# Two transformer layers on one core: block 0's projections by token tile, two single loads of X, normalization on either of two engines, and a new order list

## The chip, the cores and the metric

The kernel runs on one core of a Trainium2 chip. The metric is the device time of one execution in microseconds (us); the time of a version is the median of its runs. The engines are PE (TensorE: matmuls, and PEld for its weight loads), DVE (VectorE), ACT (ScalarE), POOL (GpSimd) and SP (SyncE, which here only issues DMAs). Each has its own queue and works through it in order.

## The reference

The input is a sequence of 2,048 tokens of 512 bf16 values. Two layers follow, with the same weights:

```python
x = x + A(layernorm(x))      # attention
x = x + B(layernorm(x))      # MLP
x = x + A(layernorm(x))
x = x + B(layernorm(x))

# A: qkv = x @ wqkv; 32 heads of 16; scores = q k^T / 4
mask = (i - j >= 0) & (i - j < 256)       # a sliding, causal window
p = softmax(where(mask, scores, -1e9));  return (p v) @ wo
# B: gelu_tanh(x @ w1 + b1) @ w2 + b2,  512 -> 1792 -> 512
```

The layer normalization has no weights: mean and variance over the 512 values, eps 1e-5.

## The kernel before, in words

**Tiles and blocks.** X lies in SBUF as 16 tiles of 128 tokens. The two layers are run as one stream of 32 token tiles (number 0 to 31; 16 is tile 0 in the second layer), in 16 blocks of two tiles. Within a block there are these steps:

- `layernorm` (L720): DVE takes statistics of a tile (L727, L729), adds eps (L731), POOL raises to -1/2 (L734), and DVE subtracts the mean and scales (L737). That normalized row is transposed by four PE transposes into PSUM and copied out by ACT or DVE (`evac`, L711), or, for most tiles ahead of the MLP, by DVE and DMAs through a scratch tensor (L746 to L755).
- `lnq` (L787): both tiles of a block, then Q. `proj` (L808) makes Q or K for two of the four channel blocks of 128 in one PSUM bank, with matmuls of 256 columns, that is both token tiles at once. Each reads both transposed tiles of the block (`xr`).
- `kv` (L815): K by `proj`, copied out by one DVE instruction for two channel blocks, which also separates the even from the odd heads (L824); V with matmuls of 512 columns per tile (L834).
- `attention` (L860): the scores of a block are cut into visits of 512 columns. A visit is one group of PE matmuls of 32 rows (label S below), and two exponentials of 128 x 1024 on ACT (L903). The edges of the window are masked by multiplications on DVE or POOL (L924). `pv` (L929) multiplies by V in two halves per two channel blocks, transposes and divides on DVE (and partly POOL, L994). `outproj` (L1024) follows, with the addition to X on DVE (L784), the second layer normalization, and the addition of b2 on POOL (L1033).
- `mlp` (L1046): ten jobs of two or four tiles; W1, Gelu on ACT (L1069, or in pairs by DVE and ACT at L1058 and L1061), W2 (L1076) with 14 matmuls of 512 columns for a tile, the addition to X (L784) and, in the second layer, the store of the tile (L1081).

**Loads.** SP issues, one behind the other: X tiles 0 and 1, 2 and 3, 4 to 7, b1, Wo, X tiles 8 to 15, W1, W2, b2 (L698 to L706). ACT's queue issues the three parts of Wqkv (L694). Until data is there, PE clears PSUM banks with 8 and then 5 matmuls of 512 columns on zeros (L676).

**What sets the order.** Every instruction or small group becomes a numbered node by `add`. `ORDER` (L413) is a written-out list of all node numbers; it gives each engine the order of its queue, SP's DMAs too. `TURNS` chooses, for each node that may run on two engines (`alt`), which one it takes: copies on DVE or ACT, masks and divisions on DVE or POOL. `BANKS` names the PSUM bank or banks of each node that takes some. `_List.run` (L231) goes through the list and puts times on the nodes by a cost model (constants L188 to L192; `CODE` is for the fetching of PE's instructions); these times only decide where waits are put (`_Sched.spread`, L135), not the order. A node's waits stand in its own engine's queue, so what is behind a waiting node waits as well.

Where PE goes from one shape of matmul to another (full 128 x 128, the 32-row scores, the 17-column products with V) this text speaks of a change of shape.

Of the kernel before, what the change touches and what calls it, by code (L numbers as in the profile page):

```python
# [185 lines left out]
class _List:  # L186
# [5 lines left out]
    CODE = (194.0, 256.0, 2.006, 3400.0)  # L192
# [106 lines left out]
def bass_interleave_layers__sliding_block__dense_activation_gelu__prompt_kernel(  # L299
# [72 lines left out]
    with ExitStack() as kctx:  # L372
        S_ = _Sched(nc, kctx)

        def sb(name, shape, dtype=dt.bfloat16):
# [774 lines left out]
```

## Time and profile before

| what | before |
|---|---|
| median of 3 runs | 457.03 us (456.97 to 457.27) |
| the profiled execution | 460.18 us |
| its span, first to last instruction | 458.4 us |
| mean granted TensorE clock | 0.993 |
| PE idle waits of the kind "issue" (released by nothing that the profile shows) | 2.2 us, the longest 1.7 |
| first projection, first exponential | 9.09, 15.51 us |
| last matmul's result taken up by DVE | 455.54 us |
| exponentials (L903): count, busy | 304, 286.3 us |
| masks (L924) on POOL, on DVE | 133, 129 |
| instruction packets (queue q8) | 69, 1.13 MB |

The times inside the profile are of the profiled execution; it takes 3.15 us longer than the median of the unprofiled runs. A row of the table of stretches gives, for each engine, the busy time and in brackets the number of instructions, then the clock that was granted to PE, the share of the DMA engines and the GB/s. A row of the chain of waits has its start, its length and what it was.

### The profile page before, as it was taken

To read this page: it belongs to the slowest core of one execution; us is meant where nothing else is said; L and a number is where in the kernel's file an instruction comes from. 1 tells how busy PE (TensorE), PEld (TensorE's weight loads), DVE (VectorE), ACT (ScalarE), POOL (GpSimd) and SP (SyncE) were. 2 spreads that over 40 slices of the span, in tenths; PEclk is the share of its full clock that TensorE was granted. 3 is DMA by queue.
4 is the path that set the end of the run, shared out by engine and by line. 5 is a ranking of instruction groups with operands and counts; after the bars stand their busy time and mean duration, and the time that the engine had idled before them with its cause. 6 is when DMAs were issued, how large, how long until landed. Compare 5 with 4: busy or idle time off the path is not lost.

```text
span 458.4 us, 19422 instructions
## 1 busy us (share of the span) xinstructions
PE 444.1 (97%) x8790; PEld 238.7 (52%) x8790; DVE 368.5 (80%) x749; ACT 389.7 (85%) x462; POOL 234.7 (51%) x266
## 2 busy tenths in 40 slices
PE   7999999989899999999999999999999999999997
PEld 3655655645453554645455545546464554545664
DVE  5899988999777888989889888899788888677411
ACT  2899999999789999899997999889987999792442
POOL 5377666565768266332565467754355243462400
PEclk9999999999989999999999999999999999999999
DMA  8910000001110020100120000201012002201211
GB/s 271 370 62 4 4 3 3 4 3 26 40 35 1 9 44 9 43 3 11 21 68 3 5 23 15 60 9 24 3 23 58 3 11 52 72 2 33 67 52 36
DMA packets 27839, 18.17 MB, mean 40 GB/s; under 512 B 15852, under 2 KB 27244, under 8 KB 27756
## 3 DMA queue, kind: packets, MB, share of 16 engines
q1 hardware_dynamic: 26172, 15.35, 12.8%
q8 instruction: 69, 1.13, 1.1%
q10 hardware_dynamic: 1584, 1.57, 1.0%
q14 instruction: 14, 0.11, 0.1%
HBM read 11.41 MB, written 5.51 MB: 37 GB/s over the span
## 4 chain that ended last, share of the span: by engine, by line
PE 75%; ACT 21%; DVE 1%; DMA 1%; issue 1%
PE ps L32 74%; ACT E L903 16%; ACT gT L1069 2%; ACT gT L1061 1%; PE ps L36 1%; ACT L903 1%; ACT L1061 1%; DMA X<-in_A_x_dram 1%; DVE stat L727 0%; DVE X L784 0%; DVE xn L737 0%; ACT xnTA L715 0%; DVE statmv L729 0%; DVE veps L731 0%
## 5 line engine op out<-in xcount | busy, mean ns | idle before, releaser
L903 ACT ACTIVATE E<-ps 128x1024 bf16<-128x1024 f32 x304 | 286.3, 1048 | 24.9 <-PE ps L32 24.1
L924 POOL TENSOR_TENSOR E<-E,mask 128x512 bf16<-128x512 bf16 (+1 forms) x133 | 140.3, 1070 | 91.8 <-DVE E L924 46.9
L32 PE MATMUL ps<-W_sb,gT 128*128 128x512 bf16 x448 | 120.1, 380 | 0.0
L32 PE MATMUL ps<-xnTB,W_sb 128*128 128x512 bf16 (+1 forms) x560 | 113.1, 337 | 0.0
L32 PE MATMUL ps<-xnTA,Wqkv_sb 128*128 128x256 bf16 x512 | 76.3, 279 | 1.2 <-ACT xnTA L715 0.7
L32 PEld LDWEIGHTS ps<-xnTB,W_sb 128*128 128x128 bf16 x560 | 51.6, 98 | 43.4 <-ACT E L903 3.9
L784 DVE TENSOR_TENSOR X<-X,ps 128x512 bf16<-128x512 bf16 x64 | 43.3, 681 | 33.9 <-PE ps L32 33.0
L1069 ACT ACTIVATE gT<-ps,b1T 128x512 bf16<-128x512 f32 (+1 forms) x92 | 48.5, 588 | 23.9 <-PE ps L32 23.4
L32 PE MATMUL ps<-QT,KT 32*64 32x320 bf16 (+4 forms) x2976 | 65.7, 259 | 2.9 <-ACT E L903 1.2
L734 POOL TENSOR_TENSOR rstd<-veps,mhalf 128x1 f32<-128x1 f32 x64 | 36.2, 572 | 52.2 <-DVE veps L731 50.4
L32 PEld LDWEIGHTS ps<-W_sb,gT 128*128 128x128 bf16 x448 | 39.6, 98 | 42.2 <-issue 8.4
L32 PEld LDWEIGHTS ps<-xnTA,Wqkv_sb 128*128 128x128 bf16 x512 | 47.2, 100 | 23.9 <-issue 3.1
L32 PEld LDWEIGHTS ps<-QT,KT 32*64 32x64 bf16 x2976 | 27.6, 103 | 51.1 <-ACT E L903 32.3
L924 DVE TENSOR_TENSOR E<-E,mask 128x512 bf16<-128x512 bf16 (+1 forms) x129 | 51.1, 424 | 2.5 <-ACT E L903 2.5
L32 PE MATMUL ps<-E,Va 64*17 64x128 bf16 (+3 forms) x3872 | 49.3, 230 | 3.5 <-issue 1.7
L1033 POOL TENSOR_TENSOR X<-X,b2b 128x512 bf16<-128x512 bf16 x32 | 36.6, 1153 | 30.0 <-DVE TM L994 12.4
L989 DVE STREAM_TRANSPOSE TT<-ps 128x1024 f32<-128x1024 f32 x32 | 39.9, 1248 | 13.8 <-PE ps L32 13.1
L32 PEld LDWEIGHTS ps<-E,Va 64*17 64x17 bf16 x3872 | 39.5, 85 | 19.1 <-PE ps L32 6.3
L727 DVE BATCH_NORM_STATS2 stat<-X 128x6 f32<-128x512 bf16 x64 | 43.0, 678 | 3.9 <-DMA X<-in_A_x_dram 3.4
L824 DVE TENSOR_TENSOR KT<-ps,parmask 128x1024 bf16<-128x1024 f32 x32 | 38.6, 1206 | 1.3 <-PE ps L32 1.2
L1058 DVE TENSOR_SCALAR gT<-ps,b1T 128x512 bf16<-128x512 f32 (+1 forms) x48 | 31.8, 672 | 6.9 <-PE ps L32 6.3
L32 PE MATMUL ps<-Wqkv_sb,xnTA 128*128 128x512 bf16 x128 | 36.8, 381 | 0.5 <-issue 0.5
(49 smaller groups left out, 330.0 us busy)
## 6 DMA issues: line engine op xcount, KB each, us to landing
W_sb<-in_B_w_dram SPq DMA_DIRECT2D x2, 1792.0 KB, 17.5
scr_x<-xs_ SPq DMA_DIRECT2D x104, 32.0 KB, 1.6
xnTB<-scr_x SPq DMA_DIRECT2D x26, 128.0 KB, 2.8
out_dram<-X SPq DMA_DIRECT2D x16, 128.0 KB, 1.7
Wqkv_sb<-in_A_wqkv_dram ACTq DMA_DIRECT2D x3, 512.0 KB, 7.5
X<-in_A_x_dram SPq DMA_DIRECT2D x1, 1024.0 KB, 12.2
X<-in_A_x_dram SPq DMA_DIRECT2D x2, 256.0 KB, 4.6
X<-in_A_x_dram SPq DMA_DIRECT2D x1, 512.0 KB, 8.8
```

The lines of the kernel that those rows point to most:

```text
L32: return self.e.matmul(*a, **k)
L727: add("dve", lambda e, B: e.bn_stats(stat6[:, k6, :], X[:, t, :]), 590, reads=["X%d" % t], writes=["st%d" % k6], prio=prio)
L734: add("pool", lambda e, B: e.tensor_tensor(out=rstd[:, k : k + 1], in0=veps[:, k : k + 1], in1=mhalf[:], op=ALU.pow), 535, reads=["ve%d" % ...
L784: add("dve", lambda e, B: e.tensor_tensor(out=X[:, t, :], in0=X[:, t, :], in1=ps[:, B[g][0], :], op=ALU.add), d_psum(512), reads=["X%d" % ...
L824: add("dve", lambda e, B, g=g, i=i: e.tensor_tensor(out=KT[:, kb, :, 2 * i : 2 * i + 2, :].rearrange("p a c q -> p a (c q)"), in0=ps[:, B[ ...
L903: add("act", lambda e, B, g_=g_, gi=gi: e.activation(E[:, 2 * gi : 2 * gi + 2, e0 : e0 + 512], ps[:, B[g_][0] : B[g_][0] + 2, :], AF.Exp, ...
L924: op = lambda e, B, Ew=Ew, Mw=Mw: e.tensor_tensor(out=Ew, in0=Ew, in1=Mw, op=ALU.mult)
L989: add("dve", lambda e, B: e.transpose(TT[:, s].rearrange("p a c q d -> p a (c q d)"), ps[:, B[g][0] : B[g][0] + 2, :].rearrange("p a n -> ...
L1033: add("pool", lambda e, B: e.tensor_tensor(out=X[:, t, :], in0=X[:, t, :], in1=b2b[:], op=ALU.add), 1110, reads=["X%d" % t, "b2b"], writes ...
L1058: add("dve", lambda e, B, g=g, fc=fc: e.tensor_scalar(out=gT[:, fc, 0:M], in0=ps[:, B[g][0], 0:M], scalar1=b1T[:, fc : fc + 1], scalar2=No ...
L1061: add("act", lambda e, B, fcs=fcs: e.activation(gT[:, fcs[0] : fcs[-1] + 1, 0:M], gT[:, fcs[0] : fcs[-1] + 1, 0:M], AF.Gelu_apprx_tanh, sc ...
L1069: add("act", lambda e, B, g=g, fc=fc: e.activation(gT[:, fc, 0:M], ps[:, B[g][0], 0:M], AF.Gelu_apprx_tanh, bias=b1T[:, fc : fc + 1], scal ...
```

## The change

1. **Block 0's Q and K.** For block 0 only, each of the four channel blocks gets a PSUM bank of its own, and its matmuls are done per token tile: 128 columns for tile 0, which wait only for the transposed tile 0, and 128 columns for tile 1. There are 64 matmuls of 128 columns in the place of 32 of 256, four copies of Q of 256 columns in the place of two of 512, and four K copies of half the width in the place of two.
2. **Loads.** X 0 and X 1 are two DMAs. The second group of clearing matmuls has 7 in the place of 5.
3. **Normalization.** The subtract-and-scale of L737 may run on POOL; the new `TURNS` puts 39 of 64 there.
4. **Last tile.** W2 for tile 31 is done in two halves of 256 columns, each with its own bank, addition and store.
5. **Lists.** `ORDER`, `TURNS` and `BANKS` are new; two constants of the cost model's `CODE` and several landing times that it assumes are changed. With the new `TURNS`, 119 masks are on POOL and 143 on DVE, 22 divisions on POOL and 10 on DVE (19 and 13 before).

PE's queue in the new order begins with: 8 and 7 clears; transposes of tile 0; Q's channel blocks 0, 3 and 2 for tile 0; transposes of tile 1; Q 1, K 0 and K 1 for tile 0; Q 3, K 0 and Q 1 for tile 1; transposes of tiles 3 and 2; Q 2, K 1 and Q 0 for tile 1; block 1's first Q; V 0; the first score visit. Behind that comes K's channel blocks 2 and 3, between visits. ACT's queue has the copies of tiles 0, 1 and 3, four copies of Q, one of block 1's Q, and then the exponentials. DVE normalizes tile 0, POOL tile 1, DVE tiles 3 and 2.

```diff
-    CODE = (194.0, 256.0, 2.006, 3400.0)
+    CODE = (194.0, 256.0, 2.0090, 3700.0)
...
-        for n, took in ((8, 3420.0), (5, 1300.0)):
+        for n, took in ((8, 3420.0), (7, 1730.0)):
...
-        load_x(0, 2, 3300.0)
-        load_x(2, 2, 5500.0)
+        load_x(0, 1, 3200.0)
+        load_x(1, 1, 3600.0)
+        load_x(2, 2, 5700.0)
...
-            add("dve", lambda e, B: e.tensor_scalar(
+            scale = lambda e, B: e.tensor_scalar(
                 out=xn[:, s, :], in0=X[:, t, :], scalar1=statmv[:, k, 0:1], scalar2=rstd[:, k : k + 1],
...
+            add("dve", scale, 325, reads=["X%d" % t, "mv%d" % k, "rs%d" % k], writes=["xn%d" % s], prio=prio, lock=True,
+                alt=(("pool", scale, 760.0),))
...
+            if b == 0:
+                for kc in range(DC):
+                    g = "q0_%d" % kc
+                    prio = base + pair[kc // 2]
+                    first_proj(g, 0, kc, prio)
+                    evac(lambda B, kc=kc: QT[:, kc, 0:256], lambda B, g=g: ps[:, B[g][0], 0:256], 256,
+                         ["ps:" + g], ["Q0_%d" % kc], prio, free=[g], kind="q", boot=True)
+                return
...
+        def first_proj(g, which, kc, prio):
+            for j in range(2):
+                pe_group(g, [(Wqkv_sb[:, dc, which * D + kc * P : which * D + (kc + 1) * P], xnTA[:, 0, dc, j * P : (j + 1) * P],
+                              slice(j * P, (j + 1) * P), dc == 0, dc == DC - 1) for dc in range(DC)],
+                         P, DC, ["xa0_%d" % j, "Wqkv%d" % which], prio, fresh=(j == 0))
...
+            for kc in range(DC if b == 0 else 0):
+                g = "k0_%d" % kc
+                prio = kprio + pair[kc // 2]
+                first_proj(g, 1, kc, prio)
+                add("dve", lambda e, B, g=g, kc=kc: e.tensor_tensor(
+                    out=KT[:, 0, :, kc, :], in0=ps[:, B[g][0], 0:256][:, None, :].to_broadcast([P, 2, 256]),
+                    in1=parmask[:, :, None].to_broadcast([P, 2, 256]), op=ALU.mult), d_psum(512) + 10,
...
+        def last_tile(tau, i, prio):
+            t = tau % T
+            for half in range(2):
+                g = "y%d_%d" % (tau, half)
+                n = slice(half * D // 2, (half + 1) * D // 2)
+                pe_group(g, [(gT[:, fc, i * P : (i + 1) * P], W2_sb[:, fc, n], slice(0, D // 2), fc == 0, fc == FC - 1) for fc in range(FC)],
+                    D // 2, 1, [["g%d" % fc, "W2"] for fc in range(FC)], prio)
+                add("dve", lambda e, B, g=g, n=n: e.tensor_tensor(out=X[:, t, n], in0=X[:, t, n], in1=ps[:, B[g][0], 0 : D // 2], op=ALU.add),
...
+                dma(lambda e, B, n=n: e.dma_start(out[0, t * P : (t + 1) * P, n], X[:, t, n]),
```

More of the change, by code (lines that the diff above doesn't have):

```diff
@@ L692, in load_x @@
                 ["X%d" % t for t in range(t0, t0 + n)], lands)
-        for which, lands in enumerate((4700.0, 7500.0, 10400.0)):
+        for which, lands in enumerate((4900.0, 7900.0, 10800.0)):
             load(lambda e, B, which=which: e.dma_start(
@@ L697, in bass_interleave_layers__sliding_block__dense_activation_gelu__prompt_kernel @@
                 A_wqkv[:, which * D : (which + 1) * D].rearrange("(c p) n -> p c n", p=P)), ["Wqkv%d" % which], lands, eng="act")
-        load_x(0, 2, 3300.0)
-        load_x(2, 2, 5500.0)
-        load_x(4, 4, 9500.0)
-        load(lambda e, B: e.dma_start(b1raw[:], B_b1.rearrange("(c p) -> c p", p=P)), ["b1raw"], 9800.0)
-        load(lambda e, B: e.dma_start(Wo_sb[:], A_wo.rearrange("(c p) n -> p c n", p=P)), ["Wo"], 11500.0)
+        load_x(0, 1, 3200.0)
+        load_x(1, 1, 3600.0)
+        load_x(2, 2, 5700.0)
+        load_x(4, 4, 9700.0)
+        load(lambda e, B: e.dma_start(b1raw[:], B_b1.rearrange("(c p) -> c p", p=P)), ["b1raw"], 10000.0)
+        load(lambda e, B: e.dma_start(Wo_sb[:], A_wo.rearrange("(c p) n -> p c n", p=P)), ["Wo"], 11800.0)
         load_x(8, 8, 14700.0)
@@ L736, in layernorm @@
                 reads=["ve%d" % k, "mhalf"], writes=["rs%d" % k], prio=prio - 500)
-            add("dve", lambda e, B: e.tensor_scalar(
+            scale = lambda e, B: e.tensor_scalar(
                 out=xn[:, s, :], in0=X[:, t, :], scalar1=statmv[:, k, 0:1], scalar2=rstd[:, k : k + 1],
-                op0=ALU.subtract, op1=ALU.mult), 325,
-                reads=["X%d" % t, "mv%d" % k, "rs%d" % k], writes=["xn%d" % s], prio=prio, lock=True)
+                op0=ALU.subtract, op1=ALU.mult)
+            add("dve", scale, 325, reads=["X%d" % t, "mv%d" % k, "rs%d" % k], writes=["xn%d" % s], prio=prio, lock=True,
+                alt=(("pool", scale, 760.0),))
             g = "tp%d" % k
@@ L819, in kv @@
             xr = ["xa%d_0" % xs, "xa%d_1" % xs]
-            for i in range(DC // 2):
+            for kc in range(DC if b == 0 else 0):
[5 more added lines that the diff above has]
+                    in1=parmask[:, :, None].to_broadcast([P, 2, 256]), op=ALU.mult), d_psum(512) + 10,
+                    reads=["ps:" + g, "parmask"], writes=["K0_0_%d" % kc, "K0_1_%d" % kc], prio=prio, free=[g])
+            for i in range(DC // 2 if b else 0):
                 g = "k%d_%d" % (b, i)
@@ L1074, in mlp @@
                 tau = tau0 + i
+                if tau == NT - 1:
+                    last_tile(tau, i, prio2 + i)
+                    continue
                 g = "y%d" % tau
@@ L1082, in mlp @@
                         ["OUT%d" % t], reads=["X%d" % t], dur=2000.0, prio=prio2)
+        def last_tile(tau, i, prio):
[6 more added lines that the diff above has]
+                add("dve", lambda e, B, g=g, n=n: e.tensor_tensor(out=X[:, t, n], in0=X[:, t, n], in1=ps[:, B[g][0], 0 : D // 2], op=ALU.add),
+                    d_psum(D // 2), reads=["X%d" % t, "ps:" + g], writes=["XL%d" % half], prio=prio, free=[g])
+                dma(lambda e, B, n=n: e.dma_start(out[0, t * P : (t + 1) * P, n], X[:, t, n]),
+                    ["OUT%d_%d" % (t, half)], reads=["XL%d" % half], dur=1900.0, prio=prio)
         lnq(0, -1300, (20, 800))
```

424 rows, old and new, of tables (BANKS, ORDER, TURNS) are left out of this document.

## The prediction

> **What bounds the kernel now.** I read the page first, then the chain of waits, then the table of stretches, then the timeline of the two ends.
>
> ```profile
> span 458.4 us, 19422 instructions
> ...
> PE 444.1 (97%) x8790; PEld 238.7 (52%) x8790; DVE 368.5 (80%) x749; ACT 389.7 (85%) x462; POOL 234.7 (51%) x266
> ```
>
> PE is busy nearly always, but a busy PE need not stream at full rate, so the chain decides:
>
> ```profile
> 21.16 27.61 ACT E L903 x30
> ...
> 122.87 0.87 PE ps L32 x51
> 123.75 1.73 issue
> 125.47 2.11 PE ps L32 x24
> ...
> 156.40 1.03 ACT E L903
> 157.44 0.04 issue
> 157.48 2.40 PE ps L32 x55
> ```
>
> Up to about 157 us the end hangs mostly on ACT's exponentials; behind that it is PE alone. In between PE stands still for 1.73 us, and nothing that the profile shows releases it. The stretches:
>
> ```profile
> 6.05:9.46 3.41, 1.70 (x15) 0.81 (x14) 3.27 (x13) 1.19 (x2) 1.65 (x4) 1.00 1.09 349
> 9.46:12.87 3.41, 3.41 (x23) 2.61 (x21) 1.54 (x4) 0.60 (x1) 1.37 (x2) 0.50 1.10 350
> 20.00:50.00 30.00, 28.21 (x695) 16.36 (x693) 29.17 (x60) 29.91 (x34) 20.45 (x21) 1.00 0.19 60
> ...
> 122.00:125.50 3.50, 1.77 (x127) 1.21 (x103) 1.20 (x3) 1.64 (x3) 3.14 (x4) 1.00 0.34 73
> 125.50:128.90 3.40, 3.40 (x65) 2.21 (x65) 2.11 (x4) 1.94 (x2) 1.23 (x3) 0.50 0.53 134
> ...
> 160.00:420.00 260.00, 259.24 (x5398) 133.33 (x5396) 220.89 (x440) 231.90 (x261) 129.96 (x141) 1.00 0.12 25
> ```
>
> The columns are PE, PEld, DVE, ACT, POOL, the granted clock and the DMA. Two places lose time to something other than work. Twice a stretch of about 3.4 us with PE busy for only half of it (1.70 of 3.41, 1.77 of 3.50) is followed by 3.4 us at clock 0.50. From 20 to 50 us ACT has no room (29.91 of 30). From 160 to 420 us PE has none (259.24 of 260).
>
> **The head.** In before, X 0 and 1 land together 3.78 us after an issue at 0.80, so at 4.58; the projections start at 9.09, when both transposed tiles are there, and the first exponential at 15.51. Afterwards:
>
> (a) X 0 alone is 128 KB. The 128 KB stores of the output land in 1.7 us, the 256 KB load in 3.78; so it lands between 2.5 and 4.58, and I take 3.7. Its normalized row follows 2.45 us later, as in before (4.58 to 7.03): 6.15. But two more clearing matmuls stand ahead. In before 13 of them end at 6.58; at 0.22 to 0.43 each, 15 end at 7.0 to 7.4. So the first transpose starts at 7.0, not 7.09: the early load is worth 0.1 us, and the clears are late next.
>
> (b) Its evacuation on ACT takes 0.41 + 0.02 + 0.61 us more, as before, so Q's first halves start at 8.05, ahead of tile 1: three groups of four 128-column matmuls, 12 at 0.056 (0.223 for the four of a transpose) = 0.67. Then tile 1's transpose, three more groups, tile 1's evacuation at 9.1 to 9.7, and the second halves from 9.75. Tile 1's normalization on GpSimd was not seen. A one-input GpSimd row of 64 elements takes 0.245, the two-input 512-element add of L1033 1.153; between these ends I take 0.7, nearer to the middle as this has one input of 512. From 7.2 it ends at 7.9, or at 8.35; PE asks for it at 8.7, so either end is hidden, and from 1.5 us it would show.
>
> (c) The order list then asks for tiles 3 and 2, Q and K's second halves, block 1's first Q (8 x 0.109) and V 0 (4 x 0.216): PE is through at about 13.3. ACT has four 256-column evacuations of Q (0.34 each by the slope of the 512 and 256 rows of L1069) and block 1's Q (0.62) before the first exponential: 11.6 to 13.6. So the first exponential is at about 14.1: **1.4 us earlier**. This holds if PE keeps its clock. In 6.05 to 9.46 it would be busy 0.97 + 0.23 + 0.67 + 0.23 + 0.5 = 2.6 of 3.41 instead of 1.70; if the half clock came all the same, 3.5 us of work behind 9.46 costs 1.2 to 1.7 more. Bounds: 2.0 earlier, 0.2 later. SP issues one more load, so every later load is some 0.5 us later (three issues took 1.45): X 2 and 3 then land at most 0.5 late, which has cover behind the four evacuations; Wo, W1 and W2 are wanted tens of us later.
>
> **The order list.** I counted what ACT must do from the first exponential up to the point where PE alone goes on, and all PE work behind that point. Before: 122 exponentials at 0.925 (27.61 / 30 in the chain), 33 Gelus and 3 evacuations at 0.36 to 0.94, 6 table loads at 1.283 = 138.6 us; then 818 matmuls of 512 columns at 0.216, 376 of 256 at 0.109, 68 of 128 at 0.056, 90 score visits at 0.263, 42 halves of E times V at 0.637 (0.344 in the sequence's first block) and 225 changes of matmul shape at 0.094 = 291.5. Sum with 15.51: 445.6. Afterwards: 123 exponentials, 33 Gelus, 1 evacuation, 6 tables = 138.4; 800, 404, 68, 90, 42 and 226 = 290.8: 444.7. So **0.9 us less**. In the whole list PE has 5 more changes of shape (367 for 362), 0.5 us, which are in that sum; table loads stay at 17 changes. The sum is a floor: the last matmul ended at 455.5, 9.9 above it, and of these 9.9 the next paragraph names 4.2.
>
> **The standstill at 123.75.** The page counts 69 instruction packets of 16 KB; PE has 2 x 8790 instructions and 79 waits, so a packet is 256 of them. Before the stop PE took 242 in 2.26 us; around it:
>
> ```profile
> 121.30:123.56 2.26, 2.26 (x122) 1.45 (x120) 1.90 (x5) 1.90 (x4) 1.44 (x2) 1.00 0.51 109
> 123.56:125.46 1.90, 0.19 (x19) 0.00 (x0) 0.00 (x0) 0.44 (x1) 1.90 (x2) 1.00 0.13 19
> 279.09:282.48 3.39, 3.39 (x157) 2.04 (x134) 2.94 (x5) 2.84 (x4) 2.38 (x4) 1.00 0.10 17
> ...
> 133.90:136.15 2.25, 2.14 (x128) 1.38 (x131) 2.00 (x3) 2.25 (x3) 2.04 (x2) 1.00 0.00 0
> 122.00:128.90 6.90, 5.17 (x184) 3.42 (x160) 3.30 (x7) 3.58 (x5) 4.37 (x5) 0.76 0.43 103
> ```
>
> I read it as PE having run out of fetched instructions where the list is dense. In all, ACT idles for 3.32 of these 6.9 us. Along the old list the block of 256 at the stop takes 2.1 us of PE work. Along the new one none behind 20 us takes under 2.47, and behind 110 us none under 3.16. So the stop and its half clock go: **3.2 us less** (ACT's 3.32, less its usual idle 0.1). What is late next is ACT again. Against it: 133.90 to 136.15 shows 259 instructions in 2.25 us without a stop; so density alone is not enough, and another dense place can stop. For the new blocks of 3.06 to 3.2 us (three in a row at about 95 to 106 us, one at 260) I charge **0.3 us**. [...]
>
> **Normalization.** 39 of 64 move to GpSimd: DVE loses 39 x 0.43 = 16.8, gains 16 masks at 0.44; GpSimd gains 39 x 0.7 = 27 and loses 16 masks at 1.16 = 18.5. POOL stays near 55%, its idle half hides this: 0. If it took 1.15, POOL would gain 18 more of 223 idle: still hidden, except in 20 to 50 us (20.45 of 30).
>
> **The tail.**
>
> ```profile
> 455.54 0.69 DVE L784 TENSOR_TENSOR X<-X,ps 128x512 bf16<-128x512 bf16 x1 [1.74 <-PE ps L32]
> 456.25 0.33 SPq L1081 DMA_DIRECT2D out_dram<-X  x1
> ```
>
> 28 matmuls of 256 columns (28 x 0.109 = 3.05) replace 14 of 512 (3.02). The last addition is half as wide: L1058 takes 0.743 for 512 and 0.457 for 256, so 0.29 less. The last store has 64 KB; 32 KB stores land in 1.6, 128 KB in 1.7: 0.05 less. The first half's store issue (0.33) is past by then, since nine matmuls (1.0 us) stand behind its sum. **0.3 us less**, bounds 0.6 less and 0.1 more.
>
> **Sum.** 1.4 + 0.9 + 3.2 + 0.3 - 0.3 = 5.5. The profiled span goes from 458.4 to 452.9, its execution (460.18) to 454.7; the unprofiled median is 3.15 below that, 457.03 to **451.5**.
>
> **Rivals.**
> 1. The head does not do what it says: the clears or the half clock hold PE, and the first exponential stays near 15.3. Price 1.4: 452.9. For it: the clears already eat the early load. [...]
> 2. The stop at 123 has another cause, or comes back elsewhere once: 3.2 stay, 454.7.
> 3. **Slower**: PE's fetches become the bound. At the stop, a block of 256, counted along PE's instructions in the trace, took from 121.43 to 125.50, 4.06 us. If every block needed that, the new list's three near 100 us would lose 0.9 + 1.0 + 0.9, those behind 110 us together 4.7, and a half-clock stretch 1.7; less the 0.8 that before lost near 292: 8.4 more, 459.6. It decides from about 3.9 us for a block. Against it: 279.09 to 282.48 shows a block in 3.39 without a stop.
> 4. The lists are worth the same and what is won early is waited for later: 457.
>
> **How the numbers follow.** Forecast 0.50 (449.5 to 453.3: the 0.4 to 2.0 of the head, and 9.9 us above the floor that can move); rival 1 0.10; rival 2 0.17 (to 456); rival 3 0.13; rival 4 0.06; below 449.5 0.04. So the range 449.5 to 456.0 leaves out about 0.2. A measurement of this kernel tells 0.2% (0.9 us) from no change: faster 0.81, the same 0.06, slower 0.13.
>
> **What would show it.** First exponential at 14.1 (over 15: head wrong); granted clock 1.00 from 9.5 to 13; no issue wait of over 1 us on PE behind 20 us, and no 0.50 clock between 20 and 450; the last lasting turn from ACT to PE near 151; the last DVE addition about 0.45 long and the span ending 2.5 us behind the last matmul (2.9 before); POOL's normalization at 0.7. Several issue waits at 95 to 106 or 260 us would mean rival 3.

## The result, and the profile after

| what | before | after |
|---|---|---|
| median (6 runs each) | 457.49 us (456.97 to 459.23) | 478.76 us (477.50 to 480.45) |
| the profiled execution, its span | 460.18, 458.4 us | 477.66, 475.9 us |
| mean granted TensorE clock in the profile | 0.993 | 0.989 |
| first exponential | 15.51 us | 14.76 us |
| normalization on POOL | none | 39 x 2.077 us |

The changed kernel is slower: ratio 1.0461, 95% interval 1.0431 to 1.0492. The forecast was 451.5 us. Its page, with the shares of the chain that ended last by engine:

```profile
span 475.9 us, 19529 instructions
...
PE 447.1 (94%) x8838; PEld 240.1 (50%) x8838; DVE 361.3 (76%) x722; ACT 392.1 (82%) x466; POOL 300.9 (63%) x294
...
PE 51%; POOL 14%; DVE 14%; ACT 11%; DMA 4%; SPq 3%; issue 2%; DVEq 0%; POOLq 0%
```

The last line of the same view in before:

```profile
PE 75%; ACT 21%; DVE 1%; DMA 1%; issue 1%
```

No engine is fuller than before except POOL, and POOL is only at 63%. The chain tells more: before, PE and ACT held 96% of it; now POOL and DVE have 28%. The table of stretches (columns as before):

```profile
6.05:9.46 3.41, 2.25 (x21) 1.24 (x19) 1.89 (x7) 0.60 (x1) 2.63 (x2) 1.00 1.10 349
9.46:12.87 3.41, 3.34 (x52) 3.10 (x53) 2.76 (x10) 1.77 (x5) 1.07 (x2) 1.00 1.10 349
20.00:50.00 30.00, 25.17 (x639) 14.38 (x640) 28.41 (x54) 27.19 (x30) 23.67 (x21) 1.00 0.18 57
102.10:108.90 6.80, 6.09 (x62) 2.94 (x63) 2.72 (x9) 2.66 (x3) 4.06 (x5) 0.50 0.01 2
...
160.00:420.00 260.00, 253.51 (x5285) 129.75 (x5284) 209.28 (x405) 232.34 (x265) 161.08 (x152) 1.00 0.12 26
```

The half clock of the head is gone (1.00 behind 9.46). From 20 to 50 us ACT, which had no room before, idles for 2.8 us and PE for 4.8; from 160 to 420 PE idles for 6.5 us in the place of 0.8. And there is a new stretch of 6.8 us at clock 0.50. The chain up to it:

```profile
95.74 2.08 POOL xn L742
97.82 1.12 POOL X L1062
98.94 1.11 POOL E L953
100.05 0.53 POOL rstd L739
100.67 2.09 POOL xn L742
102.81 0.61 PE ps L36 x4
```

For 7 us the end hangs on one queue: POOL normalizes a tile (L742), adds a bias, masks, makes the rstd of the next tile, normalizes that, and only then can PE transpose it. Of waits of PE that nothing in the profile releases, the kind of the stop at 123.75 in before, one is left (us in all, times, the longest):

```profile
PE ps L32 <- issue: 0.4, 1, 0.4
```

The tail:

```profile
472.37 0.42 DVE L1124 TENSOR_TENSOR X<-X,ps 128x256 bf16<-128x256 bf16 x1 [0.29 <-PE ps L32]
...
473.35 0.42 DVE L1124 TENSOR_TENSOR X<-X,ps 128x256 bf16<-128x256 bf16 x1 [0.56 <-PE ps L32]
```

The last addition takes 0.42 us and the span ends 2.5 us behind its start, which is where the last matmul ends; so the prediction had it. The view of the tile xn (count: shortest, median and longest ns of one) has the number that it did not have:

```profile
L742 POOL TENSOR_SCALAR xn<-X,statmv,rstd x39: 2067/2077/2094, 7.4 to 451.0; 128x512 bf16<-128x512 bf16 x39
L742 DVE TENSOR_SCALAR xn<-X,statmv,rstd x25: 371/407/1248, 6.1 to 454.8; 128x512 bf16<-128x512 bf16 x25
```

### The profile page after: what moved, and what is told of

Same layout as the page of the kernel before. It is cut to its first block, busy times and chain, and to the rows that moved or that the text cites. A ratio compares the mean times of both kernels' runs of the same rounds, so it can differ in the third digit from the quotient of the medians.

```text
span 475.9 us, 19529 instructions
## 1 busy us (share of the span) xinstructions
PE 447.1 (94%) x8838; PEld 240.1 (50%) x8838; DVE 361.3 (76%) x722; ACT 392.1 (82%) x466; POOL 300.9 (63%) x294
## 3 DMA queue, kind: packets, MB, share of 16 engines
q1 hardware_dynamic: 26332, 15.35, 12.3%
## 4 chain that ended last, share of the span: by engine, by line
PE 51%; POOL 14%; DVE 14%; ACT 11%; DMA 4%; SPq 3%; issue 2%; DVEq 0%; POOLq 0%
PE ps L32 50%; ACT E L932 9%; POOL xn L742 8%; DVE E L953 3%; POOL E L953 3%; DMA scr_x<-xs_ 2%; SPq L756 2%; DVE TT L1018 2%; POOL rstd L739 2%; DVE KT L853 1%; DMA xnTB<-scr_x 1%; PE ps L36 1%; DVE xs_ L752 1%; POOL X L1062 1%; DVE X L790 1%
## 5 line engine op out<-in xcount | busy, mean ns | idle before, releaser
L953 POOL TENSOR_TENSOR E<-E,mask 128x512 bf16<-128x512 bf16 (+1 forms) x119 | 124.2, 1056 | 66.1 <-DVE E L953 33.6
L32 PE MATMUL ps<-W_sb,gT 128*128 128x512 bf16 (+1 forms) x462 | 121.4, 377 | 0.6 <-POOL xn L742 0.4
L742 POOL TENSOR_SCALAR xn<-X,statmv,rstd 128x512 bf16<-128x512 bf16 x39 | 81.0, 2077 | 16.6 <-DVE E L953 14.7
L32 PE MATMUL ps<-xnTA,Wqkv_sb 128*128 128x256 bf16 (+1 forms) x544 | 74.8, 273 | 2.1 <-ACT xnTA L720 0.7
L953 DVE TENSOR_TENSOR E<-E,mask 128x512 bf16<-128x512 bf16 (+1 forms) x143 | 61.3, 457 | 2.7 <-ACT E L932 2.5
L32 PEld LDWEIGHTS ps<-W_sb,gT 128*128 128x128 bf16 x462 | 41.0, 98 | 43.2 <-issue 7.9
L32 PEld LDWEIGHTS ps<-xnTA,Wqkv_sb 128*128 128x128 bf16 x544 | 48.5, 100 | 23.3 <-issue 4.0
L853 DVE TENSOR_TENSOR KT<-ps,parmask 128x1024 bf16<-128x1024 f32 x30 | 36.3, 1211 | 5.3 <-PE ps L32 5.0
```

The source lines that it names most:

```text
L32: return self.e.matmul(*a, **k)
L742: scale = lambda e, B: e.tensor_scalar(out=xn[:, s, :], in0=X[:, t, :], scalar1=statmv[:, k, 0:1], scalar2=rstd[:, k : k + 1], op0=ALU.sub ...
L853: add("dve", lambda e, B, g=g, i=i: e.tensor_tensor(out=KT[:, kb, :, 2 * i : 2 * i + 2, :].rearrange("p a c q -> p a (c q)"), in0=ps[:, B[ ...
L953: op = lambda e, B, Ew=Ew, Mw=Mw: e.tensor_tensor(out=Ew, in0=Ew, in1=Mw, op=ALU.mult)
```

## Experiments on the normalization

Theory 1: a normalization of 2.08 us on POOL makes the difference. Rival A: the new lists lose by themselves.

**All 64 on VectorE** (the changed kernel).

```diff
-                alt=(("pool", scale, 760.0),))
+                alt=(("dve", scale, 325),))
```

> The changed kernel with all 64 normalizations on VectorE; the order list stays, the 39 that were on GpSimd keep their places in it. Theory 1 (the loss is the 39 normalizations on GpSimd, 2.08 us each by the trace after, where 0.7 was assumed): the time falls from 478.8 to 451 to 457 us, GpSimd's busy time from 301 to about 220. Rival A (the new order, the halves or the early projections cost the time themselves): the time stays above 468.

Measured: 470.32 us (4 runs), ratio to before 1.0222 (1.0162 to 1.0282). The time is on the rival's side: the new list without POOL's help loses too. Its chain has 24% DVE for before's 1%, so this run moves the load rather than removing it; it can't tell how the list would do with a short instruction on POOL.

**The same 39 on GpSimd in the old list** (the kernel before, its own order).

```diff
-            add("dve", lambda e, B: e.tensor_scalar(
+            there = k in ON_POOL    # the 39 of the new TURNS
+            add("pool" if there else "dve", lambda e, B: e.tensor_scalar(
```

> The kernel before with the same 39 normalizations on GpSimd, in the places that its own order list gives them, and nothing else changed. Theory 1: slower than before by 12 to 35 us (470 to 492), each GpSimd normalization at 2.08. Rival A: within 4 us of before (up to 461).

Measured: 491.35 us (4 runs), ratio 1.0724 (1.0694 to 1.0753). This one edit costs 33 us in the old list, more than the whole change; the instruction takes 2.077 us here as well. That is what theory 1 expected.

**A shorter instruction in the new list, four doses.** The first two change the form: one operation (the mean is not subtracted), and two operations on constants (nothing is normalized on POOL).

```diff
-                alt=(("pool", scale, 760.0),))
+                alt=(("pool", plain, 760.0),))
# first:  plain = tensor_scalar(xn, X, scalar1=rstd, scalar2=None, op0=mult)
# second: plain = tensor_scalar(xn, X, scalar1=0.0, scalar2=1.0, op0=subtract, op1=mult)
```

> The changed kernel, but on GpSimd the normalization has one operation with one per-partition operand (times the inverse deviation; the subtraction of the mean is left out there). If the 2.08 us are the price of two operations, one takes 1.0 to 1.1 and the time falls to 455 to 462. If they are the price of the form whatever the number of operations, it stays at 2.0 to 2.1 and the time at 476 to 481.

> The changed kernel, but on GpSimd the two operations have constants in place of the two per-partition operands (minus 0, times 1: the normalization itself is left out there). If the per-partition operands are what makes 2.08 us, the instruction takes 0.6 to 1.1 and the time falls to 453 to 462; if it is the two operations, it stays at 2.0 to 2.1 and the time at 476 to 481.

The other two normalize 176 and then 64 of the 512 columns, with xn zeroed once at the start:

```diff
+            short = lambda e, B: e.tensor_scalar(
+                out=xn[:, s, 0:176], in0=X[:, t, 0:176], scalar1=statmv[:, k, 0:1], scalar2=rstd[:, k : k + 1],
+                op0=ALU.subtract, op1=ALU.mult)
```

> The changed kernel, but on GpSimd the normalization covers the first 176 of the 512 values of a row (the other 336 are left out there; the buffer is zeroed once at the start). By the rows so far (0.245 us for 64 values, 1.927 for 512 with constants, 2.077 with per-partition operands) one should take about 0.75 us, what the change's cost model and the prediction assumed. Theory 1 (only the size of this one term was wrong; head, list, stop and tail hold): 449 to 455 us. Rival A (the new list is slower by itself): above 459. Four durations, 2.08, 1.93, 1.57 and this one, then give the time as a function of the duration.

> The changed kernel with GpSimd's normalization cut to 64 of the 512 values of a row (448 left out there): by the 3.33 us per 1,000 values between 176 and 512 values (0.957 and 2.077 us) one takes 0.58 us, less than the 0.76 of the change's cost model. Theory 1 (only the size of that term was wrong): 449 to 455 us. Theory 3 (the new list is worth no more than the old one even when the normalization is as short as it assumed, because the places won are lost again to fetches and to late transposed rows): 457 to 461.

| POOL's instruction | us of one | median | ratio to before |
|---|---|---|---|
| as changed: two operations, per-row scalars, 512 columns | 2.077 | 478.76 | 1.0461 (1.0431 to 1.0492) |
| two operations on constants | 1.927 | 474.09 (2 runs) | 1.0337 (1.0308 to 1.0366) |
| one operation | 1.570 | 465.64 (2 runs) | 1.0153 (1.0112 to 1.0193) |
| as changed, 176 columns | 0.957 | 461.32 (9 runs) | 1.0044 (1.0022 to 1.0066) |
| as changed, 64 columns | 0.583 | 459.72 (10 runs) | 1.0036 (1.0021 to 1.0052) |

The median falls with the duration, the order being the same: from 2.077 to 0.583 us it is 19.0 us. (Runs of before beside them had medians of 457.5 to 458.6. The two middle doses read no mean, or neither mean nor rstd, but the waits are made from the node's list of reads, which is as in the changed kernel.) The slope is steep at the long end: the 39 x 0.15 = 5.9 us of POOL's time from 2.077 to 1.927 bring 4.7. It is flat at the short one: the 14.6 us from 0.957 to 0.583 bring 1.6, and the intervals of these two ratios overlap. The expectations on the form missed: neither operation nor operand alone is the price. The 176 columns took longer than the 0.75 us expected, and both short doses missed theory 1's 449 to 455 us. The row of the dose nearest to the one that the forecast used:

```profile
L749 POOL TENSOR_SCALAR xn<-X,statmv,rstd x39: 577/583/592, 7.5 to 434.4; 128x64 bf16<-128x64 bf16 x39
```

So with 0.58 us, less than the 0.7 that was forecast, the new list is still no faster than the old one. Theory 1 explains 19 us of the 27 between forecast and result; 8 are left for the following. By which way the duration acts is not taken apart. Beside its place in POOL's queue there is another: DVE's 125 masks of 512 columns take 0.473 us on average in the changed kernel and 0.430 in the run with 64 columns, which is 5 us of DVE's time (in the old list, 109 of them take 0.440 before and 0.493 with the 39 on POOL).

## Experiments on the fetching of instructions

**Forty idle matmuls in the old list.** Two clears are replaced by 42 matmuls of 16 columns, in the head, where PE waits anyway: 80 more PE instructions.

```diff
-        for n, took in ((8, 3420.0), (5, 1300.0)):
+        for n, pad, took in ((8, 0, 3420.0), (3, 42, 1300.0)):    # pad: matmuls of 32 x 16
```

> The kernel before, its lists untouched; two of the 13 clearing matmuls are replaced by 42 very small ones while PE waits for data, so PE's queue is 80 instructions longer ahead of everything and every 256-instruction block begins 80 instructions earlier in the work. Theory 2 (the stop at 123 us was a fetch: a block that PE works off faster than the next arrives): along the list, blocks that now hold 1.4 to 2.4 us of work stand near 90, 142, 152, 162, 175, 253, 263, 290, 309 and 385 us; issue waits appear there, the one at 123 goes, and the time rises by 5 to 16 us (463 to 474). Rival B (fetching is hidden; the stop had another cause): the time stays within 1.5 us of before and the stop stays at 123.

Measured: 476.9 us (4 runs), ratio 1.0371 (1.0339 to 1.0403). The waits of PE put down to issue (us in all, times, the longest; before: 2.2, 2, 1.7 in the second line):

```profile
PEld ps L32 <- issue: 44.1, 135, 2.4
...
PE ps L32 <- issue: 13.4, 13, 2.2
```

The stop at 123 is gone, and there are others, of 1.1 to 2.2 us, at 48, 105, 114, 172, 325, 346 and 428 us. The same work, shifted by 80 instructions against the blocks of 256, costs 17 us, a little more than expected. Of the places that the expectation named, only the one at 175 has one of these stops within 5 us.

The two traces show what the stops are. Count PE's records in order of their start (weight loads, matmuls, waits): both stops of before (123.75 and 292.11) come where the count leaves 193 when divided by 256, and so do all twelve issue waits of 0.3 us and more in the chain of this run. In each of the 14, PE goes on 1.3 to 1.6 us after a 16 KB packet of the instruction queue has been moved (1.52 and 1.27 us in before); where the block's packet was there 1.4 us or more ahead, neither trace has such a stop. How much work a block holds does not decide it: here blocks of 2.25 and 2.66 us (up to 298.2 and 288.5) pass without a stop, and the one ahead of the stop of before took 3.7.

So before stops at two of the borders of its 69 packets, and this list at twelve.

**A whole block.** 128 extra matmuls, 256 instructions:

```diff
+        for n, pad, took in ((4, 0, 1700.0), (1, 136, 3000.0)):
```

> The kernel before with 128 more matmuls in the same place (136 very small ones for 8 clearing ones), 256 instructions, one whole block: the blocks begin at the same work as in before. Theory 2: issue waits as in before (one near 123, a short one near 292) and the time of before plus what the longer start costs (read from the first exponential, 0 to 4 us). Rival C (it is the added instructions themselves that cost, not where the blocks begin): more than the padding with 40.

Measured: 459.54 us (10 runs), ratio 1.0018 (0.9997 to 1.0038), with the stop back, as its chain shows:

```profile
123.69 1.44 issue
```

So it isn't the number of instructions that costs, but where in the order the blocks begin.

## Experiments on single parts, in the old list

**Last tile in halves** (part 4 alone).

> The kernel before with the last tile's W2 in two halves and nothing else changed. Prediction's term: 0.3 us faster (0.6 faster to 0.1 slower); the last DVE addition takes about 0.45 us and the span ends about 2.5 us behind the last matmul. Rival: 0.1 slower, because the two stores' fixed time does not fall.

```diff
+        ORDER[-2:] = [3292, 3293] + list(range(3294, 3310))
+                if tau == NT - 1:
+                    last_tile(tau, i, prio2 + i)
+                    continue
```

Measured: 458.24 us (12 runs), ratio 0.9986 (0.9967 to 1.0004): some 0.6 us less, an interval that has the forecast 0.3 in it, and no gain that is told from none. In its profile the head ran at full clock (1.00 from 9.46 to 12.87, for before's 0.50) and the first exponential came at 14.26, with the head of before unchanged (15.51).

**The same, with 10 and with 5 idle matmuls in the head**, to move the blocks out of the stop at 123.

> Before with the last tile in halves and ten very small matmuls behind the clears: PE's 256-instruction blocks begin 20 instructions earlier in the work, so that the dense stretch near 121 us is split between two blocks. Theory 2 (fetches): the stop near 123 us gets shorter or goes. If a block takes about 3.4 us to arrive, the sum over the list is 2 to 3 us less: 455 to 456.5. If it takes 3.7 or more, other blocks (near 254, 264 and 275 us) lose more than is won: 460 to 463. Rival B (no fetch): 458.2 as without the ten.

> As the one with ten, with five (10 instructions). At 3.4 us for a block: 1 us less than without (457.0); at 3.7: 0.5 more (458.7). Rival B: 458.2.

Measured: 464.2 us (6 runs), ratio 1.0145 (1.0118 to 1.0171); and 459.91 us (8 runs), 1.0051 (1.0034 to 1.0069). Both are above what was expected (463 and 458.7 at most). No gain: the stop moves and multiplies. The chain of the first of the two:

```profile
100.00 0.95 issue
...
185.48 0.80 issue
...
280.42 1.68 issue
```

**X 0 and X 1 in two loads** (part 2 alone).

```diff
-        load_x(0, 2, 3300.0)
+        load_x(0, 1, 3200.0)
+        load_x(1, 1, 3600.0)
```

> Before with X 0 and X 1 in two loads and nothing else. Prediction's view: the early load alone is worth 0.1 us or less, and X 2 and 3 land up to 0.5 us later with cover behind them: within 0.3 us of before. Theory 4 (the trace after shows statistics of tile 3 waiting 1.5 us for X): the later landing of X 2 and 3 has no cover and the first exponential and the end come 0.3 to 1.5 us later.

Measured: 461.43 us (6 runs), ratio 1.0089 (1.0064 to 1.0114), some 4 us more than before and beyond both expectations; the first exponential is at 16.78. The stretches of its head:

```profile
6.05:9.47 3.42, 0.59 (x8) 0.42 (x8) 2.00 (x10) 0.60 (x1) 0.65 (x1) 1.00 1.10 349
9.47:12.88 3.41, 2.72 (x21) 2.06 (x19) 2.26 (x6) 0.60 (x1) 2.06 (x3) 0.72 1.10 349
```

X 0 is there at 3.10 (before: both at 4.6), but X 1 at 5.44 and X 2 at 8.21. DVE's queue has the statistics of tile 1 ahead of the normalization of tile 0, so tile 0's row, done at 6.87, waits for the second load; PE then idles 2.1 us for tile 1, and the granted clock is 0.72 from 9.47 to 12.88. All six executions ran below clock 1.00 (0.989 to 0.996), while 14 of the 19 of before on the same chip had 1.000. So this part costs, and in the changed kernel the two more clears and the work by token tile stand against it: PE is busy for 2.25 us of that stretch there, not 0.59.

## Experiments on what was still open

The run with 64 columns had its 15 clears behind the zeroing of xn, so its first transpose is at 8.13 us (7.07 in the changed kernel), by the experiment itself. The first of the four was to mend that, and the second and the last build on it; all three leave out 448 of 512 columns of the normalization on POOL.

**Thirteen clears and two idle matmuls** in the place of 15 clears.

```diff
-        for n, took in ((8, 3420.0), (7, 1730.0)):
+        for n, pad, took in ((8, 0, 3420.0), (5, 2, 1730.0)):
```

> The kernel of the run before (GpSimd normalizes 64 of 512 columns, xn zeroed at the start) had 15 clearing matmuls that began at 2.31 us, behind the zeroing of xn, and ended at 8.1, so that its head is 1.1 us later than that of the changed kernel (first transpose 8.13 for 7.07). Here two of the 15 clears are replaced by two matmuls of 16 columns, so the number of PE instructions stays. Theory: the head's delay passes on, since ACT's exponentials follow one another from the head on: 458.6 to 459.1 in the place of 459.7. Rival: what is won in the head is waited for later, as at the DMA wait at 129 us: 459.5 or more. The output is not the reference's, since most columns are not normalized.

Measured: 458.82 us (10 runs), ratio to before 1.0032 (1.0016 to 1.0048). That is the ratio of the run with 15 clears (1.0036); of the 0.9 us between the medians, half is the difference of before on the two occasions. The median lies in the expected range by luck, as the edit did not do what it was for: the first transpose is still at 8.13, the first exponential at 15.23 (15.35). From there the head is as forecast, though: 7.1 us from the first transpose to the first exponential, with tile 1's row in time; the changed kernel takes 7.7. Further on, a piece of its chain:

```profile
121.56 0.63 DVE Va L732
122.19 0.61 DVE xs_ L769
...
124.38 1.54 SPq L773
...
125.96 1.62 DMA scr_x<-xs_
...
128.10 3.06 DMA xnTB<-scr_x
```

Tiles 4 to 29 are transposed for W1 by DVE (xs_), four DMAs to a scratch tensor and one back. From the start of that piece to the landing 9.6 us go by, and PE stands waiting for it. The waits of the whole run (us in all, times, the longest), of matmuls and of weight loads:

```profile
PE ps L32 <- DMA xnTB<-scr_x: 2.0, 2, 1.7
PEld ps L32 <- DMA xnTB<-scr_x: 3.0, 3, 1.9
```

The two lines see the same gaps (the largest ends at 131.20 in both), so they do not add up: PE loses 2 to 3 us. In before there is one such wait, 0.5 us of a weight load. The 6.0 us in four waits, from which the next run's expectation starts, are such a sum too (2.6 and 3.4).

**W1 without that wait**: it reads columns of the weight W1 in the place of the DMA-transposed tiles; and the same edit in the kernel before.

```diff
+            far = 4 <= tau0 < NT - 2
+            xr = [] if far else ["xb%d_%d" % (js, i) for i in range(n)]
+            # operand: W1_sb[:, dc, 0 : n * P] if far, else xnTB as before
```

> As e13, and W1 reads columns of the weight W1 itself for the tiles that are transposed by DVE and DMA (4 to 29), in the place of the transposed tiles; the transposes and DMAs still run, but nothing waits for them. In the run with 64 columns PE stood idle 6.0 us for these tiles (four waits, the longest 2.5 us at 129), in before 0.5. Theory 5: what the new list lost against the forecast is these waits: 6.0 less in PE's stretch, of which I expect 4 or more to be kept: 453 to 455. Rival: ACT or another wait is late next and the end moves by less than 1.5: 457.5 or more. In between: partly.

> The control: the kernel before, with the same edit of W1's operand. PE waited for these tiles for 0.5 us in the profile of before. Theory 5: the old list has nothing to win here: 0 to 0.7 less than before (457.3 to 458.3 where before is 458). Rival: taking the waits out gains 2 us or more in any list, for instance because the operand is read at another place: 456 or less; then the gain of e14 says nothing of the new list.

Measured: 455.77 us (10 runs), ratio 0.9958 (0.9943 to 0.9972); the control 457.48 us (10 runs), 1.0001 (0.9982 to 1.0021). The new list gains 3.05 us by it, the old one nothing. So the waits are on the path, about as long as the weight loads' 3.0 us; the expected 4 were too many, and the rival's "less than 1.5" too few.

**X 0 and 1 in one load**, in the new list:

> As e13, but X 0 and 1 come in one load again. In the changed kernel DVE's queue has the statistics of tile 1 ahead of the normalization of tile 0, so tile 0's row waits for the second load (5.29 us) though its own landed at 3.15; in before the common load landed at 4.6. Theory: loading apart costs in this list too, some 0.7 us for X 1 and 1.3 for X 2 and 3 (8.06 for 6.9): 0.5 to 1.3 less than e13. Rival: the new list needs the early X 0, or its clears hold the head anyway: within 0.4 of e13.

```diff
-        load_x(0, 1, 3200.0)
-        load_x(1, 1, 3600.0)
+        load_x(0, 2, 3300.0)
```

Measured: 458.39 us (10 runs), ratio 1.0026 (1.0004 to 1.0047), 0.4 less than with two loads; the intervals of the two overlap, so nothing is settled here, but that the early X 0 brings nothing to this list that can be measured. In both runs the clears end at 8.1 only and would hide it. The first exponential moves from 15.23 to 15.12.

## Why the prediction was wrong

**The normalization, "0", is the step that failed.** The term was 39 x 0.7 = 27 us on POOL, hidden by its idle half. It measured 39 x 2.077 = 81 us, and 19.0 of the 27 us between forecast and result go with this duration. Two things were wrong in it. The bounds: 0.245 us for 64 columns of two operations on constants was put down as the lower end for 512 columns without counting columns. Eight times 0.245 is 1.96, and that form measured 1.927 at 512. The row that it rests on, in before:

```profile
L660 POOL TENSOR_SCALAR mask<-mask 128x64 bf16<-128x64 bf16 x1 | 0.2, 245 | 0.0
```

The upper end, the addition of 1.153, was no end at all: even one operation with a scalar for each row, on one input, measured 1.570. The normalization itself takes 2.077 us there against 0.407 on DVE. And the cover: "the idle half" is a share of the span, but the instruction is a link between statistics and transpose, in one queue with masks, biases and the rstd of the next tile. The text's own limit was right: "from 1.5 us it would show". (Its balance of POOL also leaves out two masks of 256 columns and three divisions that moved to POOL, some 4.5 us; the argument does not change by them.)

**The sum of 5.5 was wrong too**, hidden by the first error. With the short instruction the list stands at 458.8, 7.3 above the forecast:

- 3.05 us are waits for the DMA-transposed tiles (shown by the pair of runs with W1 freed and their control). The prediction looked for what is late behind the stop and named ACT; it is a chain of DVE, SP and DMAs, which the count of ACT's and PE's work doesn't contain. Rival 4, "what is won early is waited for later", at 457 with a chance of 0.06, is the case that fits this list best. The waits alone do not make the whole 7.3.
- Up to 1.1 us is the later first transpose of these runs (8.13 for 7.07), an estimate, as no run took it out.
- The head's 1.4 us and 1.7 of the stop's 3.2 came from two half-clock stretches of the profiled execution. They were then subtracted from the median of executions which, for the most part, do not have them: two such stretches lower the mean clock to 0.993, and 62 of the 85 executions of before beside the experiments had 0.999 or 1.000. On the chip that shows all three, their medians are 457.83 us at full clock (16 executions), 459.62 at 0.996 (10) and 460.69 at 0.993 (2), so the 3.15 us by which the profiled execution was above the median are about what two stretches cost. Four profiles of the old head at full clock (two with 5 and 10 idle matmuls in it) have the first exponential at 13.71 to 14.26, so the forecast 14.1 is 0.2 earlier than these at best and 0.4 later at worst; and the stop without its half clock, 1.44 to 1.48 us in such profiles, is all that they have of the 3.2. That makes 2.9 to 3.5 us of gain that was not there to be had: the 3.15 came off twice. It is read from profiles and from the clocks of executions; no run takes it apart.

The three come to 7.1 to 7.7, with estimates in the last two. With the 3.15 taken off once, the sum of 5.5 gives the 454.7 that the prediction has for the profiled execution, and the first two make up the 4.1 from there to 458.8. In the changed kernel itself X 0 landed early (3.15) and was worth nothing, as in (a); tile 1's row in (b) was ready at 9.45 and not at 7.9, and the first exponential came 0.7 us later than in (c).

**The stop.** It was read as a fetch, and that is shown: 80 instructions move it, 256 bring it back (1.44 us at 123.69), and PE goes on 1.3 to 1.6 us after a packet has been moved. The reason given for it, a block of 2.1 us, is not: counted from border to border that block took 3.7 us, and shorter ones pass. Why a packet comes late stays open. In the changed kernel the stop is gone as forecast, with 0.4 us as PE's longest issue wait, and it does not come back with the normalization at 64 columns (0.2). Rival 3, fetches as the bound, is not what slowed the changed kernel, but its price for a block is real: the padded old lists pay 2 to 17 us. It had the right sign for the wrong reason.

**Half clock.** Between 20 and 450 us none was expected. There are 6.8 us from 102.1 and 3.4 from 136.2, each behind a wait of PE: 2.5 us for POOL's normalization, and 1.7 us for a copy on DVE that stood, in the chain, behind another such normalization. PE was busy for 1.18 of the 3.10 us ahead of the first and for 1.52 of the 3.20 ahead of the second, so each follows a stretch with PE busy for half of it or less, about like the two of before (1.70 of 3.41 and 1.77 of 3.50), but with another cause of the wait. That half clock always follows such a stretch is not shown: the old head, with PE busy for 1.20 of 3.41 us from 6.05 in the profile with the tail in halves, kept clock 1.00 behind it.

**The order list's 0.9** can't be judged by itself; what is shown is that waits take more than that away. One of its prices is misread: 27.61 / 30 is 0.920, not 0.925, which enters both sums alike. **The tail's 0.3** is in the interval of its own run, and its rows came out as forecast (0.42 us, 2.5 us to the end).

The range ended at 456 because no rival had the normalization above 1.15 us. A bound that counted columns would have put 39 x 1.96 = 76 us on POOL, and a rival with it.

## What to carry to other kernels

Before an operation goes to another engine, scale the nearest row of that engine by its elements and operations (here 8 x 0.245 = 1.96 us for a measured 1.927), and call nothing a bound that was measured at another size; then ask which chain the instruction is a link of, as an engine's idle share hides no link (POOL, busy for 63%, held 14% of the chain). Take a gain off the executions that have the loss: a half clock or a stop that only the profiled execution shows is not in the median. And a list that fits PE and ACT more tightly hands the path to the next slow chain, here a transpose by way of DVE, SP and DMAs (3.05 us).

## What the runs showed of the hardware that was not expected

- POOL's tensor_scalar with two per-row scalars takes 0.583, 0.957 and 2.077 us for 64, 176 and 512 columns: 3.33 ns for a column and 0.37 us besides. One operation with one such scalar takes 1.570 at 512, two on constants 1.927. DVE takes 0.407 for the same.
- In two traces PE stops 14 times at the border of a block of 256 instructions, and goes on 1.3 to 1.6 us after a 16 KB packet of the instruction queue has been moved. The time of one and the same work depended on where these blocks begin. Ratios to before: 1.0371 with 80 idle instructions more, 1.0018 with 256; with the tail in halves 0.9986, 1.0051 and 1.0145 with 0, 10 and 20 more. A change to a list moves these borders too, and that alone (17 us with 80 instructions) may be worth more than the change.
- DVE's masks of 512 columns take 0.473 us on average in the kernel whose POOL normalizes 512 columns, and 0.430 in the one where it normalizes 64, with the same list.
- Loading 128 KB alone brings it 1.5 us earlier (3.10 for 4.6), but the next 128 KB some 0.8 us later (5.44 for 4.6) and the third load by over 1 (8.21; before reads it at 6.95).
